# Sliding-window attention beside a gated MLP: SyncE's order of transposes and loads, the shape of chunk 0's k matmuls, and the start of the first q weight transfer

## The chip, the core and the metric

The kernel runs on one core of a Trainium2 chip. The metric is the device time of one execution in microseconds; lower is better. A profiled execution adds a span, from the first to the last instruction, which is a little shorter than that time.

## The reference

One layer norm feeds two branches whose results are added to the input. Shapes: x is 2048 x 640, 32 heads of 20, MLP width 1536, all in bf16.

```
xn  = layernorm(x)                                   # 2048 x 640
q, k, v = split(xn @ wqkv)                           # 32 heads of 20 each
# each position s looks at the 8 positions s, s-2, ..., s-14 (masked below 0)
a   = softmax(q[s] . k[s - 2w] * 20**-0.5, over w = 0..7)
att = (sum over w of a[w] * v[s - 2w]) @ wo
mlp = ((xn @ w_gate) * (xn @ w_up)) @ w_down
out = x + att + mlp
```

## The kernel before

The 2048 rows are cut into 16 tiles of 128 rows, numbered 0 to 15, and four chunks of four tiles (chunk 0 is tiles 0 to 3, chunk 1 tiles 4 to 7). A chunk goes through these stages:

- **norm** (lines 378 to 473). SyncE loads a tile of x (`x_t`, L258, five buffers). VectorE does two `bn_stats` (L386, L392, tile `st`), an aggregate (L398) and an addition (L399, tile `mv`). GpSimd raises to the power -1/2 (`rstd`, L406). VectorE writes the normalized tile (`xn_t`, L415). Chunk 0's tiles are turned by TensorE (`pst`, L448) and copied by ScalarE into `xnT` (L468); the other chunks' are turned by a transposing DMA on SyncE's queue (L436).
- **q and k** (`qk_group`, L483). Matmuls `psqk` (L493) with `wq` or `wk` as the stationary operand; ScalarE evicts to `qkT` (L510). Chunk 0 works tile by tile in 128 columns, for q and k alike; the other chunks in 512 columns.
- **v** (`v_tile`, L527). Matmuls `psv` (L537) with weights `wv`. `wv` is a permuted copy, made by GpSimd in five slices (`perm`, L303) of the value weights that SyncE loads into the tile `wo`, used here under the name `wr`. The first psv waits for the fifth slice. ScalarE evicts to `v_t` (L551) and GpSimd's queue stores to HBM (`vD`, L559).
- **logits** (L614). VectorE multiplies q with shifted k (`pw`, L641, 16 products a chunk in two groups of eight), TensorE sums over a head (`lps`, L661), ScalarE copies, SyncE turns (`lg`, L691), VectorE takes the maximum, ScalarE the exponential, VectorE the sum.
- **attend** (`attend`, L749, for each tile). SyncE loads the eight shifted rows of v (`v8`, L757, 1280 KB, two buffers), VectorE multiplies (L771) and adds (L782 and on) into `o16`, SyncE turns that into `oT` (L794).
- **gu** (L568) and **project** (L804). The MLP's matmuls `psg` and `psu` (L579), evictions (L594), the product `hT` (L603); then `psd` accumulates `oT` with `wo` (L834) and `hT` with `w_down` (L841), VectorE adds x (L864) and a DMA stores (L875).

No engine's order is written by hand. Every operation is a `Step` with a cost, dependencies, a priority and the buffers that it takes. `Plan.run` (L76) is a list scheduler on the host: it keeps a clock for each engine, places the step that can start first, and emits it, so the plan's estimates fix the order of instructions on each engine and each DMA queue. `Plan.ready` (L53) gives a step's start, with the line

```python
            at = max(at, slots[n - 1])
```

for a step that needs a buffer: it can start as soon as the plan frees one. At run time each engine works strictly in the emitted order and waits on semaphores.

Before the first transposes TensorE runs 12 matmuls on zeros (`warm`, L361, tile `wps`, operands from `zt`) and three more behind tile 0's transposes. At the start ScalarE loads its activation table (L197), with a copy of one column that makes it do so, and issues the transfer of the first 256 columns of `wq`; SyncE issues x tiles 0 to 3, the other 384 columns of `wq`, the value weights, `wk`, and further tiles of x (L278 to L293). GpSimd's queue carries `wg`, `wu` (L320) and later weights.

Of the kernel before, what the change touches and what calls it, by code (L numbers as in the profile page):

```python
# [9 lines left out]
ACT = mybir.ActivationFunctionType  # L10
# [20 lines left out]
class Plan:  # L31
# [21 lines left out]
    def ready(self, s):  # L53
        at = 0.0
        for d in s.deps:
            if d.end is None:
                return None
            gap = 0.0
            if d.eng != s.eng and s.tight:
                gap = self.hop  # L60
            elif d.eng != s.eng:
                gap = self.guard.get((d.eng, s.eng), self.hop)
            at = max(at, d.end + gap)
        if s.nbytes and s.eng != "POOL" and len(self.landed) >= 8:
            at = max(at, self.landed[-8])
        need = {}
        for t in s.takes:
            need[t.pool] = need.get(t.pool, 0) + 1
        for p, n in need.items():
            slots = sorted(self.free[p])  # L70
            if len(slots) < n:
                return None
            at = max(at, slots[n - 1])
        return at

    def run(self):  # L76
# [40 lines left out]
def kernel(  # L117
# [53 lines left out]
    with tc.manual_schedule():  # L171
# [18 lines left out]
            out=mb[:], in_=mb[:], pattern=[[DIL, W], [0, H]],  # L190
            compare_op=ALU.is_ge, fill=-1e9, base=-HALO, channel_multiplier=1,
        )
        zt = const.tile([P, D], bf16, name="zt")
        nc.vector.memset(zt[:], 0.0)

        table = const.tile([P, 1], bf16, name="table")
        nc.scalar.copy(table[:], zt[:, 0:1])  # L197


        wq = const.tile([P, KT, D], bf16, name="wq")  # L200
        wk = const.tile([P, KT, D], bf16, name="wk")
# [51 lines left out]
        def load_x(t):  # L253
            T_x[t] = token("x")

            def fn(q):
                G["x", t] = tl("x_t", [P, D], bf16, 5)
                q.dma_start(  # L258
                    out=G["x", t][:], in_=x_flat[t * P : (t + 1) * P, :]
                )  # L260

            S_x[t] = dma(fn, P * D * 2, takes=[T_x[t]])
# [12 lines left out]
            )  # L275


        S_wq = []  # L278
        for cols, q in ((slice(0, 2 * P), "ACT"), (slice(2 * P, D), "SP")):
            if q == "SP":  # L280
                for t in range(CH):
                    load_x(t)
            S_wq.append(
                load_w(
                    wq[:, :, cols],
                    A_wqkv[:, cols].rearrange("(i p) f -> p i f", p=P),
                    q,
                )
            )
        S_wr = load_qkv(2, wr)  # L290
        S_wk = load_qkv(1, wk)
        for t in range(CH, 2 * CH):
# [4 lines left out]
        )  # L297


        S_wv = None  # L300
        for i in range(KT):
            def perm(i=i):
                nc.gpsimd.tensor_copy(  # L303
                    wv[:, i, :].rearrange("p (j h) -> p j h", j=Dh, h=H),
                    wr[:, i, :].rearrange("p (h j) -> p j h", h=H, j=Dh),
                )

            S_wv = add("POOL", 1.28, perm, [S_wr, S_wv], 0.5 + 0.01 * i)

# [24 lines left out]
                prio + 0.01, deps,  # L334
            )

        load_gu(0, 0.515, [S_wr])
        S_late = []

        def load_late():  # L340
# [20 lines left out]
        def warm(n):  # L361
            def fn():
                if "wps" not in G:
                    G["wps"] = psum_l.tile([P, 512], f32, name="wps", tag="pl")
                for _ in range(n):
                    nc.tensor.matmul(
                        G["wps"][:], lhsT=zt[:, 0:P], rhs=zt[:, 0:512],
                        start=True, stop=True,
                    )

            return fn

        S_w = add("PE", 5.0, warm(12), (), -9000.0, takes=[T_w], reads=[T_w])


        S_xnT, T_xnT, S_tr = {}, {}, {}

        def norm(c, ttl, p0):
            t = c * CH + ttl
            if t not in S_x:  # L380
                load_x(t)
            T_st, T_xn, T_pt = token("st"), token("xn"), token("pt")

            def half():
                st = tl("st", [P, 2, nc.vector.BN_STATS_DIM], f32, 4)
                nc.vector.bn_stats(st[:, 0, :], G["x", t][:, 0:HS])  # L386
                G["st", t] = st

            s1 = add("DVE", 0.42, half, [S_x[t]], p0, takes=[T_st])

            def other():
                nc.vector.bn_stats(G["st", t][:, 1, :], G["x", t][:, HS:D])  # L392

            s1 = add("DVE", 0.42, other, [s1], p0)

            def stats():
                mv = tl("mv", [P, nc.vector.BN_AGGR_DIM], f32, 4)
                nc.vector.bn_aggr(mv[:], G["st", t][:])  # L398
                nc.vector.tensor_scalar_add(mv[:, 1:2], mv[:, 1:2], EPS)  # L399
                G["mv", t] = mv  # L400

            s1 = add("DVE", 0.33, stats, [s1], p0)

            def rstd():
                rs = tl("rstd", [P, 1], f32, 4)
                nc.gpsimd.tensor_tensor(  # L406
                    rs[:], G["mv", t][:, 1:2], half_t[:], ALU.pow
                )
                G["rstd", t] = rs

            s2 = add("POOL", 0.55, rstd, [s1], p0)

            def xnorm():
                xn = tl("xn_t", [P, D], bf16, 3)
                nc.vector.tensor_scalar(  # L415
                    xn[:], G["x", t][:],
                    scalar1=G["mv", t][:, 0:1], scalar2=G["rstd", t][:],
                    op0=ALU.subtract, op1=ALU.mult,
                )
# [24 lines left out]

            def tr():
                pst = psum_t.tile([P, KT, P], bf16, name="pst", tag="pt")
                for g in range(KT):
                    nc.tensor.transpose(  # L448
                        pst[:, g, :], G["xn", t][:, g * P : (g + 1) * P], ident[:]
                    )  # L450
                G["pst", t] = pst

            takes, deps = [T_pt], [s3]
            if ttl == 0:
                T_xnT[c] = token("xnT")
                takes.append(T_xnT[c])
            else:
                deps.append(S_tr[c])
            s4 = add("PE", KT * mm128, tr, deps, p0, lag=0.15, takes=takes,
                     reads=[T_xn], tight=c == 0)  # L460
            S_tr.setdefault(c, s4)
            if t == 0:
                add("PE", 0.65, warm(3), [s4], -8000.0, reads=[T_w])

            def cp():
                if ("xnT", c) not in G:
                    G["xnT", c] = tl("xnT", [P, KT, CS], bf16, 2)
# [15 lines left out]
        def qk_group(c, js, cols, prio):  # L483
# [16 lines left out]

            tts = range(cols.start // P, cols.stop // P)
            deps = [S_xnT[c, q] for q in tts]
            deps += S_wq[: 1 if max(js) < 2 else 2] if min(js) < KT else []
            deps += [S_wk] if max(js) >= KT else []
            m = add("PE", len(js) * KT * (0.003 + n / 2400.0), mm, deps, prio, lag=0.15,
                    takes=[T], reads=[T_xnT[c]], tight=c == 0)
# [20 lines left out]
        def v_tile(c, ttl, prio):  # L527
# [3 lines left out]
            for n in range(2):  # L531
                T = token("ps")

                def mm(n=n):
                    ps = psum.tile([P, 512], f32, name="psv", tag="ps")
                    for i in range(KT):
# [5 lines left out]
                        )  # L542
                    G["psv", t, n] = ps

                m = add("PE", KT * mm320, mm, [S_xnT[c, ttl], S_wv], prio, lag=0.15,
                        takes=[T], reads=[T_xnT[c]])

                def ev(n=n):
# [334 lines left out]

        for ttl in range(CH):
            norm(0, ttl, -2000.0 + ttl)
        for ttl in range(CH):
            cols = slice(ttl * P, (ttl + 1) * P)
            for a, js in enumerate(([0, 1], [2, 3, 4], [5, 6, 7], [8, 9])):
                qk_group(0, js, cols, 10.0 + ttl + 0.1 * a + (2.05 if js[0] >= KT else 0.0))
        for ttl in range(CH):  # L890
            v_tile(0, ttl, 14.0 + ttl)

# [68 lines left out]
```

## Time and profile before

| | |
|---|---|
| runs | 268.76, 266.65, 268.93 us; median 268.76 |
| profiled execution | 267.29 us, span 265.6 us |
| TensorE busy | 259.9 us, 98% of the span |
| VectorE busy | 212.6 us, 80% |
| ScalarE busy | 105.6 us, 40% |
| GpSimd busy | 37.1 us, 14% |
| granted TensorE clock | 1.000 |
| HBM | 35.39 MB read, 5.26 MB written |

PE is TensorE's matmuls, PEld its weight loads, DVE is VectorE, ACT ScalarE, POOL GpSimd, SP SyncE; a q behind the name is the engine's sequencer, which issues DMAs. A line such as `L303 POOL COPY wv<-wo 128x640` names the line of the kernel, the engine, the operation, what is written from what, and the shape. In a timeline the first two numbers are the start and the duration in us; in brackets stands how long the engine was idle before, and what ended that.

### The profile page before, as it was taken

To read this page: it belongs to the slowest core of one execution; us is meant where nothing else is said; L and a number is where in the kernel's file an instruction comes from. 1 tells how busy PE (TensorE), PEld (TensorE's weight loads), DVE (VectorE), ACT (ScalarE), POOL (GpSimd) and SP (SyncE) were. 2 spreads that over 40 slices of the span, in tenths; PEclk is the share of its full clock that TensorE was granted. 3 is DMA by queue.
4 is the path that set the end of the run, shared out by engine and by line. 5 is a ranking of instruction groups with operands and counts; after the bars stand their busy time and mean duration, and the time that the engine had idled before them with its cause. 6 is when DMAs were issued, how large, how long until landed. Compare 5 with 4: busy or idle time off the path is not lost.

```text
span 265.6 us, 4798 instructions
## 1 busy us (share of the span) xinstructions
PE 259.9 (98%) x1888; PEld 152.8 (58%) x1906; DVE 212.6 (80%) x331; ACT 105.6 (40%) x192; POOL 37.1 (14%) x60
## 2 busy tenths in 40 slices
PE   7999999999999999999999999999999999999995
PEld 3896654444456467744467547644457764445775
DVE  5399979999999929999998369999982999992221
ACT  2666365665543551045512463055551105555000
POOL 5596652150003000000000002000000000000000
PEclk9999999999999999999999999999999999999999
DMA  6979899359999872259899402897811129722111
GB/s 200 381 217 231 228 393 373 81 157 282 240 261 257 233 120 100 69 152 271 245 202 266 102 0 83 254 255 224 252 21 22 49 77 247 222 49 52 49 49 52
DMA packets 52786, 46.60 MB, mean 175 GB/s; under 512 B 25038, under 2 KB 50844, under 8 KB 52764
## 3 DMA queue, kind: packets, MB, share of 16 engines
q1 hardware_dynamic: 49580, 36.58, 52.8%
q0 software_dynamic: 2384, 9.34, 10.6%
q10 hardware_dynamic: 800, 0.38, 0.5%
q8 instruction: 15, 0.25, 0.4%
q14 instruction: 7, 0.06, 0.1%
HBM read 35.39 MB, written 5.26 MB: 153 GB/s over the span
## 4 chain that ended last, share of the span: by engine, by line
PE 82%; DMA 9%; DVE 5%; SPq 1%; issue 1%; DVEq 0%
PE psd L841 20%; PE psu L579 19%; PE psg L579 19%; PE psd L834 8%; PE psqk L493 8%; DMA x_t<-in_A_x_dram 6%; PE psv L537 5%; DMA xnT<-xn_t 3%; PE lps L661 3%; DVE pw L641 2%; DVE st L386 1%; DVE st L392 1%; SPq L258 1%; SPq L266 1%; DVE xn_t L415 1%
## 5 line engine op out<-in xcount | busy, mean ns | idle before, releaser
L579 PE MATMUL psu<-xnT,wu 128*128 128x512 bf16 x236 | 59.3, 379 | 0.2
L579 PE MATMUL psg<-xnT,wg 128*128 128x512 bf16 x231 | 58.7, 379 | 0.5
L841 PE MATMUL psd<-wd,hT 128*128 128x320 bf16 (+2 forms) x396 | 58.1, 295 | 0.0
L641 DVE TENSOR_TENSOR pw<-qkT 128x1280 bf16<-128x1280 bf16 x64 | 49.4, 824 | 5.0 <-ACT qkT L510 5.0
L841 PEld LDWEIGHTS <-hT 128*128 128x128 bf16 x396 | 38.0, 98 | 14.3 <-issue 0.2
L771 DVE TENSOR_TENSOR v<-v,a 128x5120 bf16<-128x5120 bf16 x16 | 45.1, 2819 | 0.3 <-DMA v<-vD 0.3
L594 ACT CAST gs<-psg 128x512 bf16<-128x512 f32 x48 | 28.1, 585 | 42.8 <-PE psg L579 41.4
L594 ACT CAST us<-psu 128x512 bf16<-128x512 f32 x48 | 28.1, 585 | 38.8 <-PE psu L579 38.8
L579 PEld LDWEIGHTS <-wu 128*128 128x128 bf16 x240 | 23.5, 98 | 27.8
L579 PEld LDWEIGHTS <-wg 128*128 128x128 bf16 x240 | 23.3, 98 | 27.7 <-issue 0.4
L510 ACT CAST qkT<-psqk 128x512 bf16<-128x512 f32 (+2 forms) x46 | 24.4, 531 | 19.8 <-PE psqk L493 19.3
L864 DVE TENSOR_TENSOR ob<-psd,xr 128x320 bf16<-128x320 f32 (+2 forms) x33 | 15.1, 476 | 17.6 <-PE psd L841 17.6
L834 PE MATMUL psd<-wo,oT 128*128 128x320 bf16 (+2 forms) x165 | 27.1, 295 | 0.0
L603 DVE TENSOR_TENSOR hT<-gs,us 128x512 bf16<-128x512 bf16 x48 | 19.2, 419 | 6.5 <-ACT us L594 6.4
L782 DVE TENSOR_TENSOR v<-v 128x2560 bf16<-128x2560 bf16 x16 | 23.7, 1484 | 0.0
L493 PE MATMUL psqk<-xnT,wq 128*128 128x128 bf16 (+1 forms) x172 | 23.1, 286 | 0.6 <-DMA wq<-in_A_wqkv_dram 0.3
L537 PE MATMUL psv<-wv,xnT 128*128 128x320 bf16 x160 | 23.1, 299 | 0.0
L493 PE MATMUL psqk<-xnT,wk 128*128 128x128 bf16 (+1 forms) x173 | 22.7, 287 | 0.1
L559 POOL DMA_DIRECT2D vD<-v_t x16 | 8.9, 560 | 86.0 <-ACT v_t L551 86.0
L834 PEld LDWEIGHTS <-oT 128*128 128x128 bf16 x165 | 16.0, 98 | 6.6
L537 PEld LDWEIGHTS <-xnT 128*128 128x128 bf16 x160 | 15.5, 98 | 7.0 <-issue 0.4
L551 ACT CAST v_t<-psv 128x320 bf16<-128x320 f32 x32 | 13.2, 429 | 13.8 <-PE psv L537 10.6
(53 smaller groups left out, 169.8 us busy)
## 6 DMA issues: line engine op xcount, KB each, us to landing
v<-vD SPq DMA_DIRECT2D x16, 1280.0 KB, 6.6
x_t<-in_A_x_dram SPq DMA_DIRECT2D x16, 160.0 KB, 5.2
vD<-v_t POOLq DMA_DIRECT2D x16, 160.0 KB, 2.5
out_dram<-ob SPq DMA_DIRECT2D x15, 160.0 KB, 2.3
wg<-in_B_w_gate_dram POOLq DMA_DIRECT2D x2, 960.0 KB, 7.3
wu<-in_B_w_up_dram POOLq DMA_DIRECT2D x2, 960.0 KB, 7.7
wd<-in_B_w_down_dram POOLq DMA_DIRECT2D x1, 1920.0 KB, 9.2
xr<-in_A_x_dram SPq DMA_DIRECT2D x11, 160.0 KB, 3.9
```

Source lines behind the costliest of these rows:

```text
L493: nc.tensor.matmul(ps[:, a * n : (a + 1) * n], lhsT=w[:, i, jj * P : (jj + 1) * P], rhs=G["xnT", c][:, i, cols], start=(i == 0), stop=(i = ...
L510: nc.scalar.copy(qk_tile(c)[:, js[0] : js[-1] + 1, HALO + cols.start : HALO + cols.stop], ps[:, 0 : len(js) * n].rearrange("p (j s) -> p j ...
L537: nc.tensor.matmul(ps[:, 0:HS], lhsT=G["xnT", c][:, i, ttl * P : (ttl + 1) * P], rhs=wv[:, i, n * HS : (n + 1) * HS], start=(i == 0), stop ...
L579: nc.tensor.matmul(ps[:], lhsT=wt[h][:, i, ff * P : (ff + 1) * P], rhs=G["xnT", c][:, i, :], start=(i == 0), stop=(i == KT - 1),)
L594: nc.scalar.copy(g[:], G["ps" + nm, c, f][:])
L603: nc.vector.tensor_tensor(hT[:], G["gs", c, f][:], G["us", c, f][:], ALU.mult)
L641: nc.vector.tensor_tensor(pt[:], qk[:, 0:KT, HALO + hh * TH : HALO + (hh + 1) * TH], qk[:, KT:, o : o + TH], ALU.mult,)
L771: nc.vector.tensor_tensor(v, v, G["a16", c][:, ttl, :, None, :].to_broadcast([P, W, Dh, H]), ALU.mult,)
L782: nc.vector.tensor_tensor(v8[:, 0:4], v8[:, 0:4], v8[:, 4:8], ALU.add)
L834: nc.tensor.matmul(G["psd", t, n][:, 0:wide], lhsT=G["oT", t][:, g, :], rhs=wo[:, g, cols], start=(g == 0), stop=False,)
L841: nc.tensor.matmul(G["psd", t, n][:, 0:wide], lhsT=G["hT", c, f][:, ttl * P : (ttl + 1) * P], rhs=wd[:, f, cols], start=False, stop=(f == ...
L864: nc.vector.tensor_tensor(G["ob", t][:, cols], G["psd", t, n][:, 0:wide], G["xr", t][:, cols], ALU.add,)
```

## The change

There are five edits.

- `Plan.ready`: a step on SyncE whose buffer is not free from the outset is placed 0.2 us (two hops) after the plan frees it, where it was placed at once. A transpose that depends on the same VectorE step as the buffer's release comes out ahead of the load that takes the buffer, for `oT` and `v8` as for `xnT` and `x_t`.
- The warm-up matmuls take their operands from a tile `zw` of 128 x 128 zeros, which VectorE clears first, and are 11 instead of 12. The moving operand repeats `zw` four times.
- ScalarE's first copy writes one column of `wq` instead of a tile of its own, so the transfer that ScalarE's queue then issues into `wq` waits for that copy, and the copy for the table. This transfer holds 384 columns instead of 256. The other 256 stand on SyncE's queue ahead of x tile 3 instead of 384 behind it.
- Chunk 0's q stays in 128 columns, with groups that fit the new split of `wq`. Its k runs in 512 columns behind the q of all four tiles.
- The permutes and the first `wg` and `wu` loads also depend on the `rstd` of tile 3, and are entered in the plan later.

In the emitted order: 15 psg matmuls stand ahead of the first psv (10 before); GpSimd's order from there is `wg` issue, rstd 4, permute 3, rstd 5, `wu` issue, rstd 6, rstd 7, permute 4, rstd 8, permute 5 (before: `wg` issue, permute 3, rstd 4, rstd 5, `wu` issue, rstd 6, permute 4, rstd 7, permute 5); 40 psv matmuls and then chunk 1's q and k follow (70 psv before). SyncE issues the first `xnT` transpose ahead of x tile 9 (behind it before), and x tiles 13 and 14 ahead of the first `v8`.

```diff
@@ Plan.ready
-            at = max(at, slots[n - 1])
+            late = s.eng == "SP" and slots[n - 1] > 0.0
+            at = max(at, slots[n - 1] + (2 * self.hop if late else 0.0))
@@ constants
+        zw = const.tile([P, P], bf16, name="zw")
+        nc.vector.memset(zw[:], 0.0)
         zt = const.tile([P, D], bf16, name="zt")
         nc.vector.memset(zt[:], 0.0)
-        table = const.tile([P, 1], bf16, name="table")
-        nc.scalar.copy(table[:], zt[:, 0:1])
@@ first loads
-        S_wq = []
-        for cols, q in ((slice(0, 2 * P), "ACT"), (slice(2 * P, D), "SP")):
-            if q == "SP":
-                for t in range(CH):
-                    load_x(t)
-            S_wq.append(load_w(wq[:, :, cols], ..., q))
+        nc.scalar.copy(wq[:, 0, 0:1], zw[:, 0:1])
+        S_wq = [load_q(slice(0, 3 * P), "ACT")]
+        for t in range(CH):
+            load_x(t)
+            if t == 2:
+                S_wq.append(load_q(slice(3 * P, D), "SP"))
@@ permutes, first gate and up weights
-            S_wv = add("POOL", 1.28, perm, [S_wr, S_wv], 0.5 + 0.01 * i)
+                S_wv.append(
+                    add("POOL", 1.28, perm, [S_wr, S_rstd[CH - 1]] + S_wv[-1:],
+                        0.5 + 0.01 * i)
+                )
-        load_gu(0, 0.515, [S_wr])
@@ warm-up
-                        G["wps"][:], lhsT=zt[:, 0:P], rhs=zt[:, 0:512],
+                        G["wps"][:].rearrange("p (a b) -> p a b", a=4), lhsT=zw[:],
+                        rhs=zw[:, None, :].to_broadcast([P, 4, P]),
-        S_w = add("PE", 5.0, warm(12), (), -9000.0, takes=[T_w], reads=[T_w])
+        S_w = add("PE", 5.0, warm(11), (), -9000.0, takes=[T_w], reads=[T_w])
@@ chunk 0
+        permute()
+        load_gu(0, 0.515, [S_wr, S_rstd[CH - 1]])
         for ttl in range(CH):
             cols = slice(ttl * P, (ttl + 1) * P)
-            for a, js in enumerate(([0, 1], [2, 3, 4], [5, 6, 7], [8, 9])):
-                qk_group(0, js, cols, 10.0 + ttl + 0.1 * a + (2.05 if js[0] >= KT else 0.0))
+            qs = ([0, 1], [2], [3, 4]) if ttl == 0 else ([0, 1, 2], [3, 4])
+            for a, js in enumerate(qs):
+                qk_group(0, js, cols, 10.0 + ttl + 0.1 * a)
+        for j in range(KT, 2 * KT):
+            qk_group(0, [j], slice(0, CS), 13.5 + 0.1 * j)
```

More of the change, by code (lines that the diff above doesn't have):

```diff
@@ L275, in load_qkv, with load_q @@
             )
-        S_wq = []
-        for cols, q in ((slice(0, 2 * P), "ACT"), (slice(2 * P, D), "SP")):
-            if q == "SP":
-                for t in range(CH):
-                    load_x(t)
[L283 to L289, printed above, removed]
+        nc.scalar.copy(wq[:, 0, 0:1], zw[:, 0:1])
+        def load_q(cols, q):
+            src = A_wqkv[:, cols].rearrange("(i p) f -> p i f", p=P)
+            return load_w(wq[:, :, cols], src, q)
+        S_wq = [load_q(slice(0, 3 * P), "ACT")]
[3 more added lines that the diff above has]
+                S_wq.append(load_q(slice(3 * P, D), "SP"))
         S_wr = load_qkv(2, wr)
@@ L297, with permute, perm @@
         )
[L300 to L305, printed above, removed]
+        S_wv = []
+        def permute():
+            for i in range(KT):
+                def perm(i=i):
+                    nc.gpsimd.tensor_copy(
+                        wv[:, i, :].rearrange("p (j h) -> p j h", j=Dh, h=H),
+                        wr[:, i, :].rearrange("p (h j) -> p j h", h=H, j=Dh),
+                    )
+                S_wv.append(
+                    add("POOL", 1.28, perm, [S_wr, S_rstd[CH - 1]] + S_wv[-1:],
+                        0.5 + 0.01 * i)
                 )
-            S_wv = add("POOL", 1.28, perm, [S_wr, S_wv], 0.5 + 0.01 * i)
         mark = const.tile([P, 1], bf16, name="mark")
@@ L371, in warm @@
             return fn
-        S_w = add("PE", 5.0, warm(12), (), -9000.0, takes=[T_w], reads=[T_w])
-        S_xnT, T_xnT, S_tr = {}, {}, {}
+        S_w = add("PE", 5.0, warm(11), (), -9000.0, takes=[T_w], reads=[T_w])
+        S_xnT, T_xnT, S_tr, S_rstd = {}, {}, {}, {}
         def norm(c, ttl, p0):
@@ L411, in norm @@
             s2 = add("POOL", 0.55, rstd, [s1], p0)
+            S_rstd[t] = s2
             def xnorm():
@@ L502, in qk_group @@
             deps = [S_xnT[c, q] for q in tts]
-            deps += S_wq[: 1 if max(js) < 2 else 2] if min(js) < KT else []
+            deps += S_wq[: 1 if max(js) < 3 else 2] if min(js) < KT else []
             deps += [S_wk] if max(js) >= KT else []
@@ L543, in mm @@
                     G["psv", t, n] = ps
-                m = add("PE", KT * mm320, mm, [S_xnT[c, ttl], S_wv], prio, lag=0.15,
+                m = add("PE", KT * mm320, mm, [S_xnT[c, ttl], S_wv[-1]], prio, lag=0.15,
                         takes=[T], reads=[T_xnT[c]])
```

## The prediction

> **What bounds the kernel now.** I read the first part of the page, then TensorE's waits, then the chain of waits, then the timeline of the first 45 us.
>
> ```profile
> PE 259.9 (98%) x1888; PEld 152.8 (58%) x1906; DVE 212.6 (80%) x331; ACT 105.6 (40%) x192; POOL 37.1 (14%) x60
> ```
>
> TensorE is busy for 259.9 of 265.6 us, so the time is the sum of its matmuls plus the moments in which it waits. Its waits (us in total, times, longest) are few:
>
> ```profile
> PE wps L366 <- DVE zt L194: 1.3, 1, 1.3
> PE psqk L493 <- DMA wq<-in_A_wqkv_dram: 0.3, 1, 0.3
> PE lps L661 <- DVE pw L641: 0.3, 1, 0.3
> ```
>
> Nothing waits for an attention output's transpose (oT), for a value load or for an eviction, so the edit on SyncE's order can win nothing there. At most the head (wps, L366) and these 0.6 us can be won; what can be lost is a new wait, since the instruction order on every engine is fixed and lost TensorE time is never made up. The likeliest place is the first value matmul (psv, L537), which needs the fifth permuted weight slice (wv, L303) from GpSimd. GpSimd's timeline (start, duration):
>
> ```profile
> 11.01 2.58 POOL L303 COPY wv<-wo 128x640 bf16<-128x640 bf16 x2 [1.56 <-DMA wo<-in_A_wqkv_dram]
> 13.53 1.04 POOL L320 DMA_DIRECT2D wg<-in_B_w_gate_dram  x1
> 14.57 1.33 POOL L303 COPY wv<-wo 128x640 bf16<-128x640 bf16 x1
> 15.86 1.09 POOL L406 TENSOR_TENSOR rstd<-mv,half_t 128x1 f32<-128x1 f32 x2
> 16.90 0.90 POOL L320 DMA_DIRECT2D wu<-in_B_w_up_dram  x1
> 18.38 0.56 POOL L406 TENSOR_TENSOR rstd<-mv,half_t 128x1 f32<-128x1 f32 x1 [0.58 <-DVE mv L399]
> 18.90 1.31 POOL L303 COPY wv<-wo 128x640 bf16<-128x640 bf16 x1
> 20.18 0.63 POOL L406 TENSOR_TENSOR rstd<-mv,half_t 128x1 f32<-128x1 f32 x1
> 20.77 1.31 POOL L303 COPY wv<-wo 128x640 bf16<-128x640 bf16 x1
> ```
>
> The last slice ends at 22.08. TensorE and VectorE at that time:
>
> ```profile
> 16.46 0.45 DVE L415 TENSOR_SCALAR xn_t<-x_t,mv,rstd 128x640 bf16<-128x640 bf16 x1
> ...
> 17.23 0.69 DVE L415 TENSOR_SCALAR xn_t<-x_t,mv,rstd 128x640 bf16<-128x640 bf16 x1
> ...
> 19.38 1.02 DVE L415 TENSOR_SCALAR xn_t<-x_t,mv,rstd 128x640 bf16<-128x640 bf16 x1
> ...
> 20.05 2.32 PE L579 MATMUL psg<-xnT,wg 128*128 128x512 bf16 x9
> ...
> 21.54 2.69 DVE L641 TENSOR_TENSOR pw<-qkT 128x1280 bf16<-128x1280 bf16 x3
> ...
> 22.21 9.67 PE L537 MATMUL psv<-wv,xnT 128*128 128x320 bf16 x70
> ```
>
> psv starts at 22.21, 0.13 us after the slice: the permutation is already as tight as it can be. And an xn_t that meets a permute is held: 0.45 us alone, but 1.02 us when the permute of 18.90 runs until 20.21; it ends 0.19 us after it. Beside the weight issue of 16.90 to 17.80 it takes 0.69.
>
> **The change, part by part.**
>
> Head. One of 12 warm-up matmuls goes (5.21/12 = 0.43 us), and the 0.33 us memset of zt shrinks to 64 words (bounds: qkT's 35 words took 0.09, zt's 320 took 0.33; I take 0.12), so the first starts 0.2 earlier. The first transposes move from 6.38 to about 5.75, and not before xn_t ends at 5.63: 0.6 us.
>
> q weights. The ACT transfer was issued at 1.31, during the table load (0.81 to 2.09); now it waits for the copy that ends at 2.29, and issues at about 2.35 with 480 KB for 320. Behind it on ScalarE stands only the first xnT copy (6.86), and no load is held on SyncE. Bounds of its landing: 4.1 us (the 320 KB on ACT) and 6.2 us (the 480 KB on SP), so 6.4 to 8.5; TensorE wants it at 6.95. In exchange the wait for the second part (until 8.87) goes. From 1.1 us gained to 0.5 lost; I take 0.5 gained. x tile 3 now stands behind 320 KB of q: from 6.13 to 8.8 at worst, its rstd done by 10.8, before the value weights land at 10.96, so no permute waits for it.
>
> k of chunk 0. 100 matmuls of 128 columns (75 in 4.35 us: 58 ns) become 25 of 512 (1.08/5 = 216 ns): 5.8 to 5.4, a gain of 0.4.
>
> So TensorE finishes q and k of chunk 0 at 20.05 - 0.5 - 0.4 = 19.15. wg landed 5.8 us after its issue of 13.53, at 19.36, and its issue stands where it stood. Then come 15 psg matmuls instead of 10 (5 x 0.216 = 1.08 us moved ahead of psv): TensorE is ready for psv at 19.4 + 3.2 = 22.6.
>
> The permutes. In the new order GpSimd runs: wg issue, rstd 4, permute 3, rstd 5, wu issue, rstd 6, rstd 7, permute 4, rstd 8, permute 5. Five rstd stand before the last permute instead of four, and each needs VectorE's statistics. x tile 4 lands where it did (13.47), since the bytes ahead of it are the same. With VectorE's rows (two statistics and the aggregate and addition behind them 1.24 us a tile, xn_t 0.45):
> - its statistics end at 14.81, rstd 4 runs until 15.45, permute 3 from 15.43 to 16.75;
> - VectorE reaches xn_t of tile 4 at 15.62, inside that permute: held to 16.94. Tile 5's aggregate, already behind it in order, ends at 17.3, rstd 5 at 17.9, the wu issue at 18.8, rstd 6 at 19.4;
> - tile 6's statistics end at 18.5, xn_t 5 meets the wu issue and ends at 18.95, tile 7's statistics end at 20.2, rstd 7 at 20.85, permute 4 runs 20.83 to 22.15;
> - VectorE does tile 8's two statistics and reaches xn_t 6 at 21.0: held to 22.35; xn_t 7 to 22.75, tile 8's aggregate to 23.1, rstd 8 to 23.75, permute 5 from 23.75 to 25.05.
>
> psv then starts at 25.1, after a new wait of 2.5 us. Before, it started at 22.21 with 1.08 us less done: 25.1 - 1.08 - 22.21 = 1.8 us lost, and the head's gains are swallowed, since they only lengthen the wait. The other bound: if no xn_t is held, the same sum ends at 23.4, a loss of 0.1. I take the held case because three rows (17.23, 19.38, 21.54) show it.
>
> SyncE's order. Each transpose now issues ahead of the load that waits for the same buffer, so a load is late by one issue (1.2 to 1.3 us). For oT the value load behind it had 0.3 us of wait in all; VectorE's idle 20% covers it, and without that cover it would cost 1.3 us each. The first psd is reached some 3 us earlier than 76.5, and oT landed at 74.8 behind a value load that it now precedes: enough. But x tile 9 also falls behind the first xnT, and that is the uncovered one:
>
> ```profile
> 17.32 8.10 DMA xnT<-xn_t
> ...
> 30.93 8.28 DMA x_t<-in_A_x_dram
> 39.23 0.49 DVE st L386
> ...
> 40.55 4.42 DVE pw L641 x6
> 45.01 0.71 PE lps L661 x17
> ```
>
> In this chain a late x tile (14, behind a value load) stops VectorE, the products (pw) behind it are late, and lps waits. The new order cures this one (x tiles 13 and 14 precede the value load): 0.3 us won. Now tile 9's statistics precede the first products. From them to the eighth product VectorE needs 14.6 us, by its rows, and lps wants that product at 25.1 + 40 x 0.1345 + 35 x 0.216 + 0.6 = 38.6: free if x tile 9 lands by 24.0. It is issued at about 18.4, behind a transpose issued at 17.0. In the pause between wg and wu (18 to 19 us) 129 packets of SyncE's queue passed beside 73 of GpSimd's; between 21 and 22, under wu, 59 beside 57. With wu now issued 1.0 later, the pause lasts until about 20, and I take tile 9 to land by 23. I add 0 to 0.7 us for the product that meets permute 5: 0.3.
>
> Beside this stands a rule of the Trainium skill, DMA: Bandwidth & Descriptors, section Queues, rings and completion order: an engine takes turns between queues packet by packet, and within a queue descriptors go in ring order. By it the transpose, in many small pieces, outlasts wu whenever it has not passed before; the trace's 59 beside 57 agrees. That is rival 1.
>
> **Sum.** 267.29 us (span 265.6 and 1.7 around it) + 1.8 - 0.3 + 0.3 = 269.1. The median shown, 268.76, lies 1.5 above the profiled execution, whose own 267.29 is inside the runs' 266.65 to 268.93; a measurement of this kernel can tell about 1%, so 0.7% slower is no change.
>
> **Rivals.**
> 1. x tile 9 is caught behind the transpose until wu has landed (slower). wu: 17.9 + 6.5 = 24.4; the transpose landed 2.0 after wu before (25.42 to 23.44): 26.4; the tile 0.5 later (as the load behind it did): 26.9. The eighth product ends at 41.5, lps waits 2.9: 271.7 us. It decides once the tile lands after about 24. For: the 8.10 us row. Against: the later wu, and 3.3 us for the fourth transpose without such company.
> 2. No hold on xn_t, or VectorE gets ahead of the permutes: psv starts when TensorE is ready, at 22.6: 22.6 - 1.08 - 22.21 = -0.7, and -0.3 at lps: 266.3 us. For: bn statistics are never held (0.48 beside a permute). Against: the three rows.
> 3. The idle time ahead of psv grows past 2.5 us (one more held xn_t, 1.3) and the array falls back to the speed of its first us, 427 ns for 512 columns against 216: for as long as that first stretch (1.33 to 6.38) half the time is lost, 2.5 us, so 269.1 + 1.3 + 2.5 = 272.9 us. No run here shows a fall. The Trainium skill, TensorE: Matmul & The Clock Gate, Part 1, says that an idle window of about 3.4 us closes the gate; by that 2.5 is short of it.
>
> **Chances.** Forecast 0.56 (its own range 267.9 to 270.0), rival 1 0.18, rival 2 0.20, rival 3 0.03, others 0.03. Range: from rival 2 to rival 1, 266.3 to 271.8. Slower by over 1% (above 270.0 on the profiled time): rivals 1 and 3 and a twentieth of the forecast, 0.24. Faster by over 1%: an eighth of rival 2 and the rest, 0.03. Within 1%: 0.73.
>
> **What would show it.** Right: an idle stretch on TensorE ahead of the first psv, ended by wv, with the fifth permute ending near 25; xn_t rows of about 1.3 us during permutes 3 and 4; no wait at the second q part; 15 psg before psv; oT landing within some 3 us. Wrong: psv starting right behind psg (rival 2); VectorE's st waiting for x_t near 23 to 27 and a wait of lps for pw near 38 (rival 1); a wait for wk or xnT ahead of chunk 1's q.

## The result and the profile after

The changed kernel takes 270.93 us in the median (269.89 to 274.68, six runs) against 267.90 for the kernel before on the same chip (266.65 to 268.93, six runs): a ratio of 1.0113, 95% interval 1.0069 to 1.0156. Two of its six executions, 273.95 and 274.68, ran at a mean granted clock of 0.994 and are not in the ratio. The forecast was 269.1 (0.7% more than the profiled 267.29). The profiled execution took 269.89 us, its span is 268.2, and the clock was 1.000 throughout: 2.6 us of span more than before.

The first part of the page, after (busy us, share of the span, instructions; then one of the DMA queues with its packets, MB and share):

```profile
PE 260.8 (97%) x1830; PEld 149.4 (56%) x1830; DVE 214.6 (80%) x332; ACT 105.9 (39%) x190; POOL 35.2 (13%) x60
...
q8 instruction: 14, 0.23, 0.4%
```

TensorE has 58 matmul records fewer (76 in the program; some records are missing). The second line looks like nothing, 14 packets of 16 KB in the whole run; the experiments come back to it. TensorE's two largest waits (us in total, times, longest):

```profile
PE psqk L499 <- DMA xnT<-xn_t: 1.8, 2, 1.1
PE psqk L499 <- DMA wq<-in_A_wqkv_dram: 1.4, 1, 1.4
```

The wait for pw ahead of lps is gone. New are a longer wait for the first q weights, and two waits for an xnT transpose that the forecast had nowhere. The timeline of the first 36 us (start, duration):

```profile
8.35 0.72 PE L499 MATMUL psqk<-xnT,wq 128*128 128x128 bf16 x10 [1.44 <-DMA wq<-in_A_wqkv_dram]
...
15.22 5.56 PE L499 MATMUL psqk<-xnT,wk 128*128 128x512 bf16 x25
...
15.23 1.42 DVE L421 TENSOR_SCALAR xn_t<-x_t,mv,rstd 128x640 bf16<-128x640 bf16 x1
...
20.50 1.31 POOL L304 COPY wv<-wo 128x640 bf16<-128x640 bf16 x1
...
20.55 1.79 DVE L421 TENSOR_SCALAR xn_t<-x_t,mv,rstd 128x640 bf16<-128x640 bf16 x2
20.62 3.40 PE L585 MATMUL psg<-xnT,wg 128*128 128x512 bf16 x15
...
23.30 1.32 POOL L304 COPY wv<-wo 128x640 bf16<-128x640 bf16 x1
23.86 5.87 PE L543 MATMUL psv<-wv,xnT 128*128 128x320 bf16 x40
29.56 5.56 PE L499 MATMUL psqk<-xnT,wq 128*128 128x512 bf16 x25
```

xn_t is held in permutes 3 and 4, and permute 5 ends at 24.62. But psv does not wait for it: 23.86 lies inside the permute, and its 40 matmuls take 5.87 us where 40 x 0.1345 are 5.38. Chunk 1's q starts at 29.56. Put on the work of the kernel before (30 psv more, 5 psg fewer) that is 29.56 + 30 x 0.1345 - 5 x 0.216 = 32.5 against 31.72: 0.8 us late.

The chain of waits shows two transposes of 6.7 and 4.5 us from issue to landing, and the timeline what they stop:

```profile
79.55 6.72 DMA xnT<-xn_t
...
145.25 4.50 DMA xnT<-xn_t
```

```profile
86.41 1.45 PE L499 MATMUL psqk<-xnT,wq 128*128 128x512 bf16 x6 [0.72 <-DMA xnT<-xn_t]
...
149.79 1.46 PE L499 MATMUL psqk<-xnT,wq 128*128 128x512 bf16 x6 [1.07 <-DMA xnT<-xn_t]
```

In chunks 2 and 3 the first q matmuls wait 0.72 and 1.07 us for the fourth transpose; before, the same transposes landed 2 to 3 us ahead of need. So of the 2.6 us, 0.8 are there when chunk 1's q starts and 1.8 come with these waits; 0.3 were won at lps, and 0.3 I did not trace.

### The profile page after: what moved, and what is told of

It reads as the page before. It is cut to its first block, busy times and chain, and to the rows that moved or that the text cites. A ratio compares the mean times of both kernels' runs of the same rounds, so it can differ in the third digit from the quotient of the medians.

```text
span 268.2 us, 4674 instructions
## 1 busy us (share of the span) xinstructions
PE 260.8 (97%) x1830; PEld 149.4 (56%) x1830; DVE 214.6 (80%) x332; ACT 105.9 (39%) x190; POOL 35.2 (13%) x60
## 4 chain that ended last, share of the span: by engine, by line
PE 70%; DVE 14%; DMA 11%; SPq 1%; issue 1%; POOL 1%; DVEq 0%; POOLq 0%
PE psu L585 15%; PE psd L847 14%; PE psg L585 13%; PE psqk L499 12%; PE psv L543 6%; PE psd L840 6%; DMA xnT<-xn_t 5%; DMA x_t<-in_A_x_dram 3%; DVE v L777 3%; DMA v<-vD 3%; PE lps L667 3%; DVE pw L647 2%; DVE xn_t L421 2%; DVE v L788 2%; DVE hT L609 1%
## 5 line engine op out<-in xcount | busy, mean ns | idle before, releaser
L585 PE MATMUL psg<-xnT,wg 128*128 128x512 bf16 x240 | 59.3, 379 | 0.0
L647 DVE TENSOR_TENSOR pw<-qkT 128x1280 bf16<-128x1280 bf16 x64 | 48.8, 817 | 6.2 <-ACT qkT L516 5.9
L516 ACT CAST qkT<-psqk 128x512 bf16<-128x512 f32 (+3 forms) x44 | 24.0, 547 | 22.4 <-PE psqk L499 21.7
L499 PE MATMUL psqk<-xnT,wk 128*128 128x512 bf16 x100 | 22.6, 379 | 0.0
L499 PEld LDWEIGHTS <-wq 128*128 128x128 bf16 x175 | 13.0, 98 | 12.4 <-issue 4.2
```

Of the source, the lines that this page charges most:

```text
L499: nc.tensor.matmul(ps[:, a * n : (a + 1) * n], lhsT=w[:, i, jj * P : (jj + 1) * P], rhs=G["xnT", c][:, i, cols], start=(i == 0), stop=(i = ...
L516: nc.scalar.copy(qk_tile(c)[:, js[0] : js[-1] + 1, HALO + cols.start : HALO + cols.stop], ps[:, 0 : len(js) * n].rearrange("p (j s) -> p j ...
L585: nc.tensor.matmul(ps[:], lhsT=wt[h][:, i, ff * P : (ff + 1) * P], rhs=G["xnT", c][:, i, :], start=(i == 0), stop=(i == KT - 1),)
L647: nc.vector.tensor_tensor(pt[:], qk[:, 0:KT, HALO + hh * TH : HALO + (hh + 1) * TH], qk[:, KT:, o : o + TH], ALU.mult,)
```

## Experiments

**First theories.** Theory 1: SyncE's new order makes the xnT transposes late, because the value load went out at 75.63 (73.57 before) ahead of three of them. Theory 2: the head's 0.8 us is the real loss, and the xnT waits only follow from it. Theory 3: the waits come from TensorE's own order.

*The changed kernel without the wait in Plan.ready.*

```diff
-            late = s.eng == "SP" and slots[n - 1] > 0.0
-            at = max(at, slots[n - 1] + (2 * self.hop if late else 0.0))
+            at = max(at, slots[n - 1])
```

> The changed kernel with the added wait in Plan.ready taken out again, so that the planner puts the value loads and the attention transposes in the order that it had before; everything else as changed. Theory 1 (SyncE's order): the loss is for the most part the two waits of TensorE for the fourth xnT transposes of chunks 2 and 3 (gaps of 1.02 us at 85.4 and 1.35 us at 148.5 in the changed kernel). The v8 load of 75.63 goes out earlier again (73.57 before), these two gaps fall below 0.5 us together, and the time falls by 1.5 to 2.4 us against the changed kernel, to about 269.0; the start of chunk 1's q stays at 29.6. Theory 2 (the head): the loss is made in the first 32 us, and the gaps only take up slack that the tail would otherwise have: the time stays within 0.6 us of the changed kernel. Theory 3 (the gaps come from TensorE's own order): the gaps stay or move to another transpose with 2 to 2.4 us in sum, and the time stays too.

Measured: 270.22 us, ratio to before 1.0122 (1.0075 to 1.0168), so no gain over 1.0113. The waits change their place; two lines of TensorE's waits:

```profile
PE psd L839 <- DMA oT<-o: 1.0, 1, 1.0
PE psqk L498 <- DMA xnT<-xn_t: 0.5, 1, 0.5
```

*The kernel before with the wait in Plan.ready alone* (the same two lines the other way round).

> The kernel before with the added wait in Plan.ready alone. Theory 1: TensorE waits for xnT transposes in chunks 2 and 3 for about 2 us in all, the wait of 0.5 us for the exponentials near 44.5 goes or stays; the time is 1.5 to 2.4 us above the kernel before, about 269.8. Theory 2: the head is the kernel before's, so the time is within 0.6 us of the kernel before. Theory 3: no gap above 0.5 us at the transposes; the time is within 0.6 us of the kernel before.

Measured: 266.62 us, ratio 0.997 (0.9947 to 0.9993): slightly faster than before, with TensorE waiting for nothing but its first zeros. Theory 1 falls: the edit to SyncE's order gains, and where it is undone TensorE waits for oT instead.

*The changed kernel without the hold on the q weights.*

```diff
-        nc.scalar.copy(wq[:, 0, 0:1], zw[:, 0:1])
+        table = const.tile([P, 1], bf16, name="table")
+        nc.scalar.copy(table[:], zw[:, 0:1])
```

> The changed kernel with ScalarE's first copy writing a tile of its own again, so that the transfer of the first 384 columns of the q weights does not wait for it. Both theories: if the hold is what made the first q matmul start at 8.35 (7.60 before), it starts at 7.4 to 7.8 now. Theory 1: that is worth up to 0.7 us at the start of chunk 1's q (29.56 in the changed kernel), and the two gaps at the xnT transposes stay with 2.4 us in all: 270.2 to 270.9. Theory 2: the hold makes the loss, and the time falls by 1.5 us or more, to 269.4 or below.

Measured: 271.11 us, ratio 1.0153 (1.012 to 1.0187), more than either theory had. The first q starts at 7.99, but x tiles 1 to 3 share the bandwidth with the earlier 480 KB, TensorE waits 2.0 us for three xn_t, and chunk 1's q starts at 30.14. The hold is no loss: without it the kernel is not faster.

*The kernel before with k of chunk 0 in 512 columns alone.*

```diff
-            for a, js in enumerate(([0, 1], [2, 3, 4], [5, 6, 7], [8, 9])):
-                qk_group(0, js, cols, 10.0 + ttl + 0.1 * a + (2.05 if js[0] >= KT else 0.0))
+            for a, js in enumerate(([0, 1], [2, 3, 4])):
+                qk_group(0, js, cols, 10.0 + ttl + 0.1 * a)
+        for j in range(KT, 2 * KT):
+            qk_group(0, [j], slice(0, CS), 13.5 + 0.1 * j)
```

> The kernel before with chunk 0's k in 512 columns alone (q in two groups of 2 and 3 feature tiles as before, k in five groups behind all of q). The k matmuls are 25 of 0.216 us in place of 100 of 0.058 us: 5.4 us for 5.8 us. Theory 1: it gains 0.4 us at the start of chunk 1's q, or nothing where the value matmuls then wait for the permuted value weights; no xnT gaps; 267.3 to 268.1. Theory 2 expects the same, unless k behind all of q is what brings the head's loss: then the start of chunk 1's q is 0.8 us later or more, and the time 268.5 or above.

Measured: 267.00 us, ratio 0.999 (0.9966 to 1.0014). A few tenths won at most, as both theories had it, but an xnT wait of 0.3 us appears here too, with the kernel before's SyncE rule and head.

**A fourth theory, from the packets.** I then looked at what the DMA engines did while the late transposes were on their way. The DMA view of the changed kernel, 82.5 to 84.5 us, in 40 slices of 0.05 us:

```profile
GB/s 266 302 282 297 271 77 138 195 287 222 297 287 620 251 287 261 282 266 271 56 20 5 0 0 0 0 0 0 0 0 0 5 10 5 10 10 5 10 10 10
...
q8 instruction: 1, 0.02, 3.0%
```

From 83.5 on, for over 1 us, almost nothing moves. In the trace a 16 KB packet of the instruction queue starts at 83.14 and takes 0.96 us; 20 packets of 256 bytes (the transposes') that start between 83.43 and 83.56 take 1.3 to 1.43 us each, where 18 ns is usual. The instruction packets number 15 in the kernel before and 14 after, and TensorE has 3794 and 3660 matmuls and weight loads: one packet for every 253 to 261 of them. Theory 4: these are TensorE's code; while one DMA engine carries such a packet, transposes spread over all of them stand still; and since the change takes away 76 matmuls with their weight loads, the packets moved from 70.85 and 94.62 to 83.14, where the xnT transposes are in flight. It predicts that only TensorE's instruction count, not its work, decides.

*The changed kernel with that count restored.* The first 11 warm-up matmuls of 512 columns become 88 of 64.

```diff
-        S_w = add("PE", 5.0, warm(11), (), -9000.0, takes=[T_w], reads=[T_w])
+        S_w = add("PE", 5.0, warm64(88), (), -9000.0, takes=[T_w], reads=[T_w])
+            nc.tensor.matmul(G["wps"][0:32, 0:64], lhsT=zw[:, 0:32], rhs=zw[:, 0:64], start=True, stop=True)   # 88 times
```

> The changed kernel with its first 11 warm-up matmuls of 512 columns cut into 88 of 64 columns (32 columns of weights), the same zeros; nothing else. That gives TensorE 77 matmuls and weight loads more ahead of all its work, about as many as the new k of chunk 0 and the twelfth warm-up matmul took away. Theory 4 (code transfers): a 16 KB transfer of the instruction queue comes about every 253 TensorE instructions; in the changed kernel one starts at 83.14 us, and the transposes of xnT in flight on the other DMA engines stand still to 84.9 with it. With 154 instructions more it starts near 70 and near 92 as in the kernel before, the wait of chunk 2 (1.02 us) falls below 0.3, the one of chunk 3 (1.35 us, behind a transfer at 141.38) below 0.5, and the time falls by 1.5 to 2.4 us, to 268.5 to 269.4. Theory 2 (the head's delay is what makes the transposes late): the waits stay with 2 to 2.4 us in all and the time stays within 0.5 us of the changed kernel.

Measured: 270.38 us, ratio 1.0111 (1.0063 to 1.0159): no gain in the time. The packets went to 70.16 and 93.21 as expected, with no standstill between 82 and 86, and chunk 3's wait was gone. But in the profiled execution the value weights landed at 11.70 (10.52 in the changed kernel), psv waited 1.3 us for wv behind its first four matmuls, and chunk 2's transposes, the last issued at 83.08 (79.55 in the changed kernel), were still waited for (0.8 us). Not decided by this run. TensorE's psv rows:

```profile
23.84 0.71 PE L554 MATMUL psv<-wv,xnT 128*128 128x320 bf16 x4
25.82 5.05 PE L554 MATMUL psv<-wv,xnT 128*128 128x320 bf16 x36 [1.26 <-POOL wv L304]
```

*The fastest kernel so far (the wait in Plan.ready alone) with 49 pairs more:* 7 of its 12 warm-up matmuls cut into 56 in the same way.

> The kernel before with the wait in Plan.ready alone, and 7 of its 12 first warm-up matmuls cut into 56 of 64 columns, so that TensorE has 49 pairs of weight load and matmul more ahead of its work; nothing else moves on any queue. Theory 4: the 16 KB transfers of the instruction queue that were at 90.92 and 146.63 come some 9 us earlier, near 82 and near 138, the xnT transposes of chunk 2 or 3 land 1 to 2 us later than without the edit, TensorE waits for them by 0.5 to 2 us in all, and the time is 0.5 to 2 us above that of the kernel with the wait in Plan.ready alone (266.6). Theory 2: no wait for xnT, and the time within 0.4 us of 266.6.

Measured: 268.21 us, ratio 1.0034 (1.0008 to 1.006) where the same kernel had 0.997 (0.9947 to 0.9993). Packets at 82.45 and 144.81 (90.92 and 146.63 before the edit), standstills right behind them, and this line among TensorE's waits, which had none:

```profile
PE psqk L506 <- DMA xnT<-xn_t: 1.0, 1, 1.0
```

Zeros cut smaller at the start cost 0.6% at 148 us. Theories 2 and 3 have no way to that, since TensorE's order is as it was and chunk 1's q starts at 29.49 (29.68 before the edit).

*The changed kernel with the q weights split as before* (256 columns held on ScalarE's queue, 384 behind x tile 3).

```diff
-        S_wq = [load_q(slice(0, 3 * P), "ACT")]
+        S_wq = [load_q(slice(0, 2 * P), "ACT")]
         for t in range(CH):
             load_x(t)
-            if t == 2:
-                S_wq.append(load_q(slice(3 * P, D), "SP"))
+        S_wq.append(load_q(slice(2 * P, D), "SP"))
```

> The changed kernel with the q weights split as before: 256 columns on ScalarE's queue (still held by ScalarE's first copy) and 384 behind the four x tiles on SyncE's. Theory of the head: the 384 columns are what brings the first q matmul to 8.35 and the fourth transposes of x to 12.14 (7.60 and 11.39 in the kernel before); with 256 the first q matmul starts at 7.6 to 7.9, the fourth transposes near 11.5, and chunk 1's q starts 0.4 to 0.7 us earlier than 29.56. Rival: the hold itself is what costs, and the first q matmul stays at 8.2 or later. By theory 4 the waits at the xnT transposes stay between 1 and 2.4 us, since TensorE's instructions are as many; the time is 270.0 to 270.9.

Measured: 270.31 us, ratio 1.0128 (1.0094 to 1.0163). The first q starts at 6.93, earlier than expected, and chunk 1's q at 29.58 behind ten psv more: the head is 1.3 us shorter. The time is not. Packets at 83.07 and 146.32 fall on the transposes, and TensorE waits 2.5 us for xnT. The split causes the head's loss; winning it back only lengthens the waits behind it.

*The kernel before with the wait in Plan.ready, k in 512 columns, and 11 of 12 warm-up matmuls cut into 88*, so with two pairs more than before.

> The kernel before with the wait in Plan.ready, chunk 0's k in 512 columns, and 11 of the 12 first warm-up matmuls cut into 88 of 64 columns, so that TensorE has two instruction pairs more than before in all. Theory 4: the gain of the wait in Plan.ready (0.8 us by its medians) and the 0.4 us of k add up, with no wait for xnT: 266.0 to 266.5. Theory 2: the same, as its head is the kernel before's; where k in 512 columns runs into the permuted value weights, 266.6.

Measured: 266.66 us, ratio 0.9981 (0.9961 to 1.0), no wait for xnT. Within the error the same as the wait in Plan.ready alone; a new wait of 0.5 us for wg takes up what k won.

*The changed kernel with both cures,* the old split and the 88 cut warm-up matmuls.

> The changed kernel with both suspects taken out: the q weights split as before (256 columns on ScalarE's queue, still held, 384 behind the four x tiles) and the first 11 warm-up matmuls cut into 88 of 64 columns, so that TensorE's code transfers come where the kernel before has them. The held transfer, k in 512 columns, the wait in Plan.ready and the permutes behind the five rstd stay. Theory 4 with the head put down to the q split: chunk 1's q at 29.6 after 50 value matmuls (as with the q split alone), code transfers near 70 and 92 in place of 83.07, near 128 in place of 146.3, waits for xnT below 0.5 us in all (2.5 with the q split alone), no stretch at half clock: 266.3 to 267.3, no slower than the kernel before. If something else of the change costs (the permutes, the hold), 268.5 or above.

Measured: 268.06 us against 268.17 for the kernel before beside it, ratio 1.003 (0.9994 to 1.0065); 266.3 to 267.3 was expected. The span of the profiled execution is 265.5, TensorE waits 0.3 us for xnT. It is 1.0% faster than with the split alone, which differs by nothing but how zeros are cut.

*The kernel with the wait in Plan.ready and k in 512 columns, now with its 12 warm-up matmuls whole* (in place of 88 small and one whole).

> The kernel before with the wait in Plan.ready and chunk 0's k in 512 columns, the 12 warm-up matmuls whole: the same as the run with cut warm-up matmuls (266.66), but for TensorE's instructions, which are 77 pairs fewer. Theory 4: the code transfers come near 82 and near 144, as in the run with k alone, into the xnT transposes of chunk 2 and the load ahead of those of chunk 3; the transposes land 1 to 2 us later, TensorE waits for them by 0.3 to 2 us in all, and the time is 0.3 to 2 us above 266.66. Against theory 4: the same time within 0.3 us and no wait for xnT.

Measured: 269.35 us, ratio 1.0049 (1.0021 to 1.0077) where the cut one had 0.9981. With the kernel of two runs before it this makes the clearest pair, since SyncE's and GpSimd's order and the head (chunk 1's q at 29.58 and 29.64) stand alike. The same DMA view, 82.5 to 84.5 us, with cut warm-up matmuls, where no instruction packet falls into it:

```profile
GB/s 123 189 287 237 297 267 302 276 297 276 297 292 292 246 584 1147 143 128 102 1229 205 102 102 156 359 333 410 410 384 410 410 384 359 256 205 230 179 128 128 128
```

and with whole ones:

```profile
GB/s 292 302 435 118 251 227 257 287 246 292 261 276 225 46 15 10 0 0 0 0 0 0 0 0 0 5 5 5 10 10 5 10 10 5 10 15 5 10 10 10
...
q8 instruction: 1, 0.02, 3.8%
```

The fourth transpose of chunk 2 lands at 84.52 in the first and at 86.19 in the second, which costs TensorE 0.2 us there. In chunk 3 this wait follows:

```profile
PE psv L550 <- DMA xnT<-xn_t: 1.7, 1, 1.7
```

A packet at 145.71 falls on those transposes, but most of this wait comes from further ahead. The last transpose of chunk 3 lands 3.3 us later than with cut matmuls (149.52, 146.22), and 2.8 us of that are there at its issue (143.04, 140.27), since VectorE is 2.8 us late from 103 us on. 1.6 us go back to chunk 2's late transposes, for which VectorE waited near 85 us, so that a value load went out at 94.19 and not at 92.61. The rest fits a second packet, at 100.28: that load, in flight, and the transpose of the logits behind it (`lg`) landed at 102.47 and 102.94, without the packet at 99.64 and 100.14. VectorE's first row behind `lg`, with cut and then with whole matmuls:

```profile
100.16 0.42 DVE L721 TENSOR_TENSOR m<-lg 128x512 bf16<-128x512 bf16 x1 [0.58 <-DMA lg<-Lsb]
```

```profile
102.96 0.43 DVE L721 TENSOR_TENSOR m<-lg 128x512 bf16<-128x512 bf16 x1 [2.96 <-DMA lg<-Lsb]
```

The two kernels with the old q split show the second part by itself: with a packet at 100.34 the value load took 8.2 us, without it 6.4, and the last transpose of chunk 3 went out at 143.49 and 141.20.

*The changed kernel once more, and beside it on the same chip the one with 88 cut warm-up matmuls,* since that run had decided nothing.

> The changed kernel itself once more, on the same chip as the next run and profiled again, since the run with cut warm-up matmuls had lost 1.2 us in its first 31 us (value weights landed at 11.70 in place of 10.52) and so did not show what moving the code transfers alone is worth. Theory 4: waits for the fourth xnT transposes of chunks 2 and 3 of 2 to 2.5 us in all, each behind a code transfer near 83 or near 141 to 146, and chunk 1's q at 29.5 to 30.7: 1.1% above the kernel before.

> The changed kernel with the first 11 warm-up matmuls cut into 88 of 64 columns, as before, on the same chip as the changed kernel itself. Theory 4: code transfers near 70, 93 and 132 again, no standstill of xnT between 82 and 86, waits for xnT below 1.1 us in all, and, where the first 31 us are as long as in the changed kernel beside it, 1.0 to 2.0 us less than that kernel. Rival: the head alone decides and the two are within 0.5 us of each other.

Measured: 270.97 us, ratio 1.0131 (1.0094 to 1.0168), and 269.43 us, ratio 1.0065 (1.0037 to 1.0093): 0.65% apart, some 1.8 us. Not all of it can be put down to the packets: four of the six executions of the first and five of the twelve of the second have a mean granted clock of 0.987 to 0.994, and those at 0.999 or 1.000, two and seven, lie 0.45 us apart in the mean. Here the changed kernel's profiled execution (268.83 us, the shortest of its six) waited for xnT by 0.7 us only, less than expected; that of its neighbour lost 3.2 us at once, to q weights that landed at 9.64, and still had 1.0 us of xnT wait.

**What follows.** Four pairs differ only in how the warm-up zeros are cut, and each favours the count that keeps the packets off chunk 2's xnT transposes and off its `lg` (95 to 103 us): 1.0034 to 0.997, 1.0128 to 1.003, 1.0049 to 0.9981, 1.0131 to 1.0065, or 0.6 to 1.0%. Only the last pair ran side by side on one chip; in the others each ratio is to the kernel before on its own chip. The first run with cut zeros, 1.0111 against 1.0113 in another series, does not; the heads of this kernel's two profiled executions differ by 1.2 us (chunk 1's q at 30.70 and 31.89), and both are longer than in the changed kernel. So for the changed kernel with its own q split the size of the effect is open, between nothing and 0.65%.

The old split gains nothing while the packets are in the way (1.0113 and 1.0131 to 1.0128); without them 1.0065 goes to 1.003, and the intervals overlap. Open stays also what the rest, the hold and the permutes, costs: the kernel with both cures is not told apart from the kernel before. And one difference was not tested: in the changed kernel's emitted order the first xnT transpose of chunks 2 and 3 stands behind an oT transpose, with the old q split ahead of it (chunk 3's goes out at 138.90 for 133.66). With the packets elsewhere the two profiled executions of the changed kernel with cut zeros still wait 0.8 and 1.0 us for xnT. The two fastest are the kernel before with the wait in Plan.ready (266.62), and that with k in 512 columns and cut warm-up matmuls (266.66).

## Why the prediction was right and wrong

- **Head.** The first transposes start at 5.73; 5.75 was forecast. Right, and worth nothing, since the next matmul waits for wq.
- **q weights.** This term was wrong in sign. The landing, 8.22, is inside the bounds (6.4 to 8.5), but I took 0.5 us gained where the first q came 0.75 later (8.35 for 7.60). With the old split it came at 6.93. I had weighed the held transfer against the cured wait for the second part, and not that the 384 columns and the second part now share the bandwidth ahead of x tile 3, which came late too (8.41 for 6.13, inside the 8.8 allowed). I asked only whether a permute would wait for that tile's rstd; its xn_t ran into the first permute (1.44 us from 10.64, 0.45 before) and held TensorE for 0.17 us at 12.14.
- **k of chunk 0.** In matmul time right: 25 in 5.40 us, from 15.22 to 20.62. But the step counted microseconds and not instructions. The 76 matmuls taken away moved TensorE's code packets onto the transposes. The sum has no term for that. The waits for xnT are the larger part of the loss, 1.8 us in the profile, and the pairs give 0.6 to 1.0% to the packets; how much of the 1.8 us is theirs in the changed kernel itself is not shown.
- **The permutes.** The mechanism was right row by row: xn_t 1.42 and held again behind permute 4, permute 5 from 23.30 to 24.62 (23.75 to 25.05 forecast). Its price was not. I let psv wait for the fifth slice as the plan has it; at run time only the fifth matmul of a group reads that slice. In the kernel before, too, psv had waited for nothing: ten psg from 20.05 take 10 x 0.216 us, to 22.21, where psv starts, and no wait for wv stands among TensorE's waits. That the slice ended 0.13 us earlier was chance, and I read it as a wait. TensorE, ready at 23.86 because of the late q, lost about 0.5 us inside psv, not 2.5. The sum of the head and this step was 0.8 us for the 1.8 forecast.
- **SyncE's order.** x tile 9 landed at 23.52 (23 taken, 24.0 the limit), and the wait of lps is gone: right. "x tile 9 ... is the uncovered one" was too narrow: the fourth xnT transposes of chunks 2 and 3 had only 2 to 3 us in hand, and I did not list them. That the edit as such costs nothing is shown; alone it gains 0.3%.
- **Rivals.** Rival 1 did not happen. Rival 2's sign came, psv right behind psg, but not its reason or its time: xn_t was held, and TensorE was ready at 23.86 and not at 22.6. Rival 3's fall of the clock came in other kernels and at other places, after a shorter idle time than it named, as the last section shows; in the changed kernel's profile the clock stays at 1.000.

So 269.1 lacked 1.8 us for late transposes and had 1.0 too much for the permutes: 269.1 + 1.8 - 1.0 = 269.9, the profiled execution. That the forecast lies 0.8 us from it is luck in part, since two errors of opposite sign in part cancel. By the medians the kernel is 1.1% slower, just outside the 1% within which 0.73 was given, and the interval excludes the "no change" of the sum. Of the signs that were named, the end of permute 5, the held xn_t, the second q part without a wait and the quick oT (2.6 to 4.0 us to landing) came; the one that carried the price, an idle stretch ahead of psv ended by wv, did not.

## What to carry to other kernels

An edit that changes only the number of TensorE's instructions can move the transfers of its code, and these share the DMA engines with the data. The wait can show far behind them: here two packets, at 83 and 100 us, stand behind most of a wait at 148. Before a large change is explained by what it was meant to do, look at what the instruction queue carries in the window of the new wait, and cut some harmless instructions smaller or larger to see whether the wait moves. List each transfer's slack, not only the waits that show: 2 to 3 us in hand is little beside a standstill of over 1 us, and a gain ahead of such a point turns into a longer wait at it.

## What the hardware showed that was not expected

**Code packets can stop transposes.** A 16 KB packet takes about 1 us (0.88 to 2.03 in these traces), by the profile's shares on one DMA engine. From 0.3 to 0.5 us after its start the packets of transposes in flight took 1.3 us and more (83.14 and 83.43 in the changed kernel, 82.45 and 82.97, 82.60 and 83.11 in two others). Not each packet does it: one at 144.08, in the kernel with cut warm-up matmuls and k in 512 columns, fell on chunk 3's transposes and only slowed them for some 0.5 us.

A packet also seems to act late: in the changed kernel a packet of 1.75 us at 141.38 fell into the value load of 140.23; at 146.75 only some 26 GB/s of its 1280-byte packets were still moving, about what one engine carries of them (one takes 55 ns), and the transposes behind it waited until 147.5. That the late engine is the one that carried the code is a guess from the order of these records; no run tested it. A standstill of the same look needs no code packet: the kernel with both cures has one in 81.5 to 83.5 us, behind a value load, with no instruction packet between 68.63 and 90.34:

```profile
GB/s 292 246 195 179 138 113 102 72 87 72 87 67 26 26 26 26 26 26 26 26 26 26 26 26 26 26 26 26 26 26 0 21 15 20 15 77 256 247 277 287
```

The Trainium skill, DMA: Bandwidth & Descriptors, section Why a DMA increments its semaphore by 16 and not by 1, says that up to 16 engines finish a transfer's parts independently and that it has landed only with the last of them; the late landings agree. That the other engines stop meanwhile is shown by the rows above alone.

**The clock can fall after a short idle time.** In the profiled execution with the old split alone TensorE was idle for 1.95 us ahead of 148.26, and for the kernel with cut warm-up matmuls in the last pair for 3.2 us ahead of 9.78. Rows by stretch (us, PE busy, PEld, DVE, ACT, POOL, granted clock, DMA share, GB/s), the first kernel and then the second:

```profile
148.00:149.00 1.00, 0.74 (x5) 0.56 (x6) 0.97 (x3) 0.00 (x0) 0.00 (x0) 0.89 1.21 329
...
150.00:151.00 1.00, 1.00 (x5) 0.50 (x4) 0.00 (x0) 0.31 (x1) 0.00 (x0) 0.50 1.28 316
```

```profile
10.00:11.00 1.00, 1.00 (x18) 1.00 (x16) 1.00 (x3) 0.47 (x2) 0.00 (x0) 0.78 1.06 360
11.00:12.00 1.00, 1.00 (x12) 1.00 (x11) 0.43 (x4) 0.76 (x2) 0.51 (x2) 0.50 1.06 365
```

By the shares of the stretches the clock goes to one half 0.5 to 0.8 us after the work resumes and stays there for some 3.4 us, which costs 1.7; one such stretch makes the mean granted clock of an execution 1 - 1.7 / 269 = 0.994. An idle time of 1.69 us in the kernel with whole warm-up matmuls did not do it. The Trainium skill, TensorE: Matmul & The Clock Gate, Part 1, has the clock fall after an idle window of about 3.4 us; here the fall came once after 1.95 us, so the measurement decides against counting on 3.4 us of idle time.
